# Sixteen half heads through two fixed slots, with wo in the third

## The chip, the core and the metric

The kernel runs on one core of a Trainium2 chip. The core has five engines with a queue each: TensorE (PE, with its weight loads shown as PEld), VectorE (DVE), ScalarE (ACT), GpSimd (POOL) and SyncE (SP), and sixteen transfer engines that move data between the main memory and the core. All arithmetic here is in 32-bit floats. The metric is the device time of one execution in microseconds, as the median of several.

## The reference

One decode step for 8 sequences. `x` is normalised; one branch is attention over a cache, the other a gated MLP; the result is `x + s * silu(b)`.

```python
def _A_ref(x, k_cache, v_cache, wq, wo):
    q = (x @ wq).reshape(8, 1, 32, 128)              # 32 query heads of 128
    k = repeat(k_cache, 4); v = repeat(v_cache, 4)   # 8 cached heads, 4096 positions
    p = softmax(einsum("bhqd,bhkd->bhqk", q, k) * 128 ** -0.5)
    return einsum("bhqk,bhkd->bhqd", p, v).reshape(8, 1, 4096) @ wo

def _B_ref(x, w_in, w_sp, b_sp, w_out):
    z = gelu(x @ w_in)                               # 512 -> 1792
    g = w_sp * layernorm(z[..., 896:]) + b_sp
    return (z[..., :896] * g) @ w_out

xn = layernorm(x)
return x + _A_ref(xn, ...) * silu(_B_ref(xn, ...))
```

(The transposes of the axes are left out.) The two caches have 8 x 8 x 4096 x 128 numbers each, 134 MB; `wq` and `wo` have 8.4 MB each.

## The kernel before

**Tiles and slots.** The cache of one head, of either kind, is cut into two halves of four sequences. A half is one tile of 128 partitions x 16384 numbers, 8.39 MB. There are three places for such tiles, slots a, b and c. `wq` begins in slot b and the MLP's weights in slot c; `wo` ends in slot a.

**Prologue** (L91 to L223). It loads `wq`, `x`, the MLP's weights and the first half of K (slot a), all on SP's queue; computes the queries and, once `wq` is used, loads the second half of K into slot b (L160); then it computes the MLP's gate. The head loop begins when the prologue has ended on all engines.

**The head loop.** TensorE runs `head_products` eight times in a hardware loop (L452). The other engines have their whole order written out: `head_sides` (DVE and ACT) and `loads` (SP) emit the instructions of every head one after the other. All waits are on semaphores: `pe` counts TensorE's steps (8 a head, `STEPS`), `dve` DVE's, `token` tells TensorE that DVE has got to a point (`tell`, `take`), and `landed_*` count transfers.

A head runs like this. Scores (L353): the two K tiles, from slots a and b, are multiplied with the queries; each product has a weight of 32 columns in one of four column strips of the array and 512 moving columns, and its records come in pairs, so 64 records for one tile. The queries of all heads lie in `qs`; `place_q` copies those of one head into `q`, a buffer of zeros with one window per sequence, so that the products of different sequences add up in disjoint rows of `sc`. Softmax: DVE takes the negated row maximum (`nm`), ACT exponentiates with the row sum (`l`), and since four strips of a row hold different stretches of positions, TensorE and DVE bring their maxima and sums together through a transpose (L357), a second transpose (L359) and a product with `same_all` (L361); DVE scales `p` and transposes it in blocks into `pT`. Values (L372): the V tile in slot c with the first four sequences, then the V tile in slot b with the others, into two banks `o_ps`. After each half DVE picks the diagonal blocks (`o_all`, `o_sb`) and TensorE folds them (L382) into `po`; two dummy products (L379), whose result nobody reads, stand ahead of the second fold. DVE copies `po` to `oT`, for the last head to `oT_last`.

**SP's order** in `loads`: V first half into slot c, V second half into slot b once the scores are done, the next head's first K half into slot a, and the next head's second K half into slot b once the second V half is used. Behind the last head it loads `wo` in six pieces (`WO_PIECES`, in units of 256 columns) into slot a and the rows of `x` for the output.

**The end** (`last_products`, `last_sides`). `wo` is 32 rows (head and repetition) of 512 columns. The first 28 (`FOLDED`) are multiplied in two halves of 256 columns, four rows side by side in the four strips (L408), and DVE and ACT copy one half each from PSUM into `part_sb` (L258 and L330). The products with `pick` (L430) add the four strips up into `acc`; the last four rows go to `acc` directly (L417), two of them ahead of the copies and two behind. DVE multiplies by the gate, adds `x`, and ACT stores. L258 is the line of the helper `v`, through which all of DVE's work in the loop goes; rows are told apart by their tiles.

Of the kernel before, what the change touches and what calls it, by code (L numbers as in the profile page):

```python
# [8 lines left out]
AX = mybir.AxisListType  # L9

# [4 lines left out]
G = 4  # L15
# [13 lines left out]
FOLDED = HKV * REP - REP  # L29
AHEAD = FOLDED + 2  # L30
# [3 lines left out]
STEPS = 8  # L34
WARM = 384


class Chip:


    def __init__(self, nc):
# [22 lines left out]
        self.q = sb("q", P, B * (R + REP))  # L64
# [6 lines left out]
        self.o_sb = [sb(f"o_sb{i}", P, DH) for i in range(2)]  # L71
        self.part_sb = [sb(f"part_sb{i}", P, D // 2) for i in range(2)]
# [9 lines left out]
        self.o_ps = [ps(f"o_ps{i}", P, G, DH) for i in range(2)]  # L82
        self.po_bank = ps("po", P, 512)
        self.po = self.po_bank[:, :B * REP]
# [6 lines left out]
def prologue(tc, t, x, w_mlp, wq, k0, k1, landed_a, landed_b):  # L91
# [31 lines left out]
    for z in [t.acc, *t.o_ps]:  # L123
        nc.vector.memset(z, 0.0)
# [35 lines left out]
    second = nc.sync.dma_start(slot_b, k1).then_inc(landed_b, 16)  # L160
# [65 lines left out]
def place_q(nc, t, h):  # L226
    return nc.vector.tensor_copy(t.q.rearrange("p (b s) -> p b s", b=B)[:, :, :REP], t.qs[:, h])


class Heads:  # L230
# [5 lines left out]
    def __init__(self, nc, t, landed_a, landed_b, stored):  # L236
# [3 lines left out]
        self.landed_a, self.landed_b, self.landed_c = landed_a, landed_b, nc.alloc_semaphore("landed_c")  # L240
# [4 lines left out]
        self.end = HKV * STEPS  # L245
        half_d = D // 2
        self.part = [t.sc[:, 0, :half_d], t.o_ps[0].rearrange("p g d -> p (g d)")[:, :half_d]]
# [16 lines left out]
    def loads(self, kT, v, wo, x_rows):  # L264
        sync, (a, b, c) = self.nc.sync, self.t.slots
        for h in range(HKV):
            at = h * STEPS
            if h:
                sync.wait_ge(self.pe, at - 8 + 7)
                sync.dma_start(b, kT[h, 1]).then_inc(self.landed_b, 16)  # L270
                sync.wait_ge(self.pe, at - 8 + 6)
            sync.dma_start(c, v[h, 0]).then_inc(self.landed_c, 16)
            sync.wait_ge(self.pe, at + 2)
            sync.dma_start(b, v[h, 1]).then_inc(self.landed_b, 16)
            sync.wait_ge(self.pe, at + 1)
            if h < HKV - 1:
                sync.dma_start(a, kT[h + 1, 0]).then_inc(self.landed_a, 16)
        for (lo, hi), landed in zip(WO_PIECES, self.landed_wo):
            sync.dma_start(a[:, lo * HD:hi * HD], wo[:, lo * HD:hi * HD]).then_inc(landed, 16)
        sync.dma_start(self.t.x_out, x_rows).then_inc(self.landed_x, 16)  # L280

    def head_sides(self, h):

        nc, t, at, v, vec = self.nc, self.t, h * STEPS, self.v, self.nc.vector
        p = t.p
        v(vec.tensor_reduce, t.nm, t.sc, op=ALU.max, axis=AX.XY, negate=True, pe=at + 2)
# [5 lines left out]
          op=ALU.min, axis=AX.X, pe=at + 3)  # L292
        v(vec.tensor_copy, t.full, t.nmin[:, None, :].to_broadcast([1, G, R]), own=True)
        self.tell()
        v(vec.tensor_sub, t.w, t.scr[1][:, :1], t.nm, pe=at + 4)
# [5 lines left out]
        v(vec.reciprocal, t.wl, t.scr[1][:, 1:2], pe=at + 5)  # L301
# [4 lines left out]
        if h < HKV - 1:  # L306
            vec.wait_ge(self.dve, self.nv)
            place_q(nc, t, h + 1).then_inc(self.dve, 1)
            self.nv += 1
        self.tell()  # L310
        for half in range(2):
            v(vec.tensor_mul, t.o_all, t.o_ps[half], t.diag[:, :, None].to_broadcast([P, G, DH]),
              pe=at + 6 + half)
            v(vec.tensor_reduce, t.o_sb[half], t.o_all.rearrange("p g d -> p d g"), op=ALU.add, axis=AX.X,
              own=True)
            self.tell()
        po_t = t.po.rearrange("p (b r) -> p r b", r=REP)
        if h < HKV - 1:
            v(vec.tensor_copy, t.oT[:, h], po_t, pe=at + 8)
        else:  # L320
            for a in range(2):
                v(vec.tensor_copy, t.oT_last[:, :, a, a * B:(a + 1) * B], po_t, pe=at + 8)
            self.tell()

    def last_sides(self, out):
        nc, t, vec = self.nc, self.t, self.nc.vector
        self.v(vec.tensor_copy, t.part_sb[0], self.part[0], pe=self.end + 1)
        self.tell()
        nc.scalar.wait_ge(self.pe, self.end + 2)
        nc.scalar.copy(t.part_sb[1], self.part[1]).then_inc(self.part1, 1)  # L330
        vec.wait_ge(self.act, self.na).then_inc(self.act, -self.na)
        self.v(vec.tensor_mul, t.gate, t.acc, t.gate, pe=self.end + 3)
# [5 lines left out]
        vec.wait_ge(self.pe, self.end + 3).then_inc(self.pe, -(self.end + 3))  # L338

    def take(self, sem, n):  # L340
        self.nc.tensor.wait_ge(sem, n).then_inc(sem, -n)  # L341

    def head_products(self):
        nc, t, step = self.nc, self.t, lambda mm: mm.then_inc(self.pe, 1)
        slot_a, slot_b, slot_c = t.slots
        for half, (slot, landed) in enumerate(((slot_a, self.landed_a), (slot_b, self.landed_b))):
            self.take(landed, 16)
            k_sb = slot.rearrange("p (i c g s) -> p i c g s", i=HALF, c=2, g=G)
            for i in range(HALF):
                b = half * HALF + i  # L350
                for c in range(2):
                    for g in range(G):
                        mm = nc.tensor.matmul(t.sc[R * g:R * (g + 1), c, :], t.q[:, b * R:(b + 1) * R],  # L353
                                              k_sb[:, i, c, g, :], start=(b == 0), stop=(b == B - 1))
# [139 lines left out]
```

## Time and profile before

| | |
|---|---|
| median of 3 runs | 678.85 us (678.63 to 678.86) |
| profiled execution | 679.39 us, of which its span is 678.1 us |
| moved by the transfer engines | 290.9 MB, 429 GB/s over the span |
| first scores on TensorE | from 61.5 us |
| last product on values, end | 665.2 us |
| store issued | 676.6 us |
| mean granted TensorE clock | 0.75 of full |

The page gives each engine's busy time and share, then the span in 40 slices: a digit is the busy share of an engine in tenths, PEclk the clock that TensorE was granted, GB/s what the transfers moved. A timeline row has the start, the duration, the engine, the line and the operation with its tiles, a count where several are merged, and in brackets the idle time ahead of it with what ended it. A group row has busy time and mean ns of one, then the idle time ahead. A row of a stretch has its bounds and length, busy time and count of PE, PEld, DVE, ACT and POOL, then granted clock, DMA share and GB/s. A transfer row has size and the median time from issue to landing. "issue" and "PEq" name an engine's own sequencer: where TensorE waits for a semaphore in its queue, for a landing above all, the idle time is written down to it.

### The profile page before, as it was taken

Reading aid. Unit: us, or ns where it says so; the run is one execution under the profiler, and the core shown is the slowest. Engines: PE = TensorE matmul, PEld = TensorE weight load, DVE = VectorE, ACT = ScalarE, POOL = GpSimd, SP = SyncE. Lnnn points to the kernel's source line nnn. Section 1 sums busy time; section 2 is a strip of 40 time slices with the busy share of each in tenths; the row PEclk is TensorE's granted clock in tenths of the full one; section 3 lists DMA queues with packets and bytes.
Section 4 is the critical chain, followed back from the end, with each engine's and each line's share of the span. In section 5 each row is a group of like instructions: output and inputs, shape, how many; then the busy total and the mean of one; then the engine's idle time right before and its main releaser. Section 6 shows DMA issues by size and latency. Waiting matters only on the chain. (4 is left out here: it accounts for less than half of the span.)

```text
span 678.1 us, 5431 instructions
## 1 busy us (share of the span) xinstructions
PE 351.0 (52%) x2480; PEld 102.7 (15%) x2480; DVE 80.7 (12%) x156; ACT 13.8 (2%) x28; POOL 2.8 (0%) x15
## 2 busy tenths in 40 slices
PE   0446743545565444456555444655645454655548
PEld 0112210111121111111111110111111111211104
DVE  0142021102110021101100021101101021100111
ACT  0010000000000000000000000000000000000000
POOL 1000000000000000000000000000000000000000
PEclk9986766778767677877766677887666678877659
DMA  9999999999999999999999999999999999999996
GB/s 383 439 433 434 434 433 433 434 433 433 433 433 433 433 433 433 437 437 437 445 437 433 437 437 433 441 437 433 433 433 433 433 433 433 433 433 433 433 414 287
DMA packets 6070, 290.90 MB, mean 429 GB/s; under 512 B 936, under 2 KB 1064, under 8 KB 1456
## 3 DMA queue, kind: packets, MB, share of 16 engines
q1 hardware_dynamic: 5920, 290.79, 99.1%
q8 instruction: 4, 0.07, 0.0%
q10 hardware_dynamic: 144, 0.03, 0.0%
q14 instruction: 2, 0.02, 0.0%
HBM read 290.78 MB, written 0.03 MB: 429 GB/s over the span
## 5 line engine op out<-in xcount | busy, mean ns | idle before, releaser
L372 PE MATMUL o_ps<-slot_b,pT 128*16 128x512 f32 x512 | 74.9, 751 | 81.0 <-PEq L341 81.0
L353 PE MATMUL sc<-slot_b,q 128*32 128x512 f32 x512 | 74.4, 746 | 73.5 <-PEq L341 73.5
L353 PE MATMUL sc<-slot_a,q 128*32 128x512 f32 x512 | 75.5, 756 | 56.2 <-PEq L341 56.2
L372 PE MATMUL o_ps<-slot_c,pT 128*16 128x512 f32 x512 | 73.9, 742 | 47.9 <-PEq L341 47.9
L258 DVE TENSOR_REDUCE nm<-sc 128x1 f32<-128x1024 f32 x8 | 9.8, 1225 | 277.0 <-PE sc L353 277.0
L258 DVE TENSOR_TENSOR o_all<-o_ps,diag 128x512 f32<-128x512 f32 x16 | 11.1, 692 | 243.4 <-PE o_ps L372 243.4
L353 PEld LDWEIGHTS sc<-slot_b,q 128*32 128x32 f32 x512 | 20.4, 134 | 127.5 <-issue 127.5
L372 PEld LDWEIGHTS o_ps<-slot_b,pT 128*16 128x16 f32 x512 | 17.6, 114 | 138.4 <-issue 138.4
L353 PEld LDWEIGHTS sc<-slot_a,q 128*32 128x32 f32 x512 | 20.7, 135 | 104.7 <-issue 104.7
L372 PEld LDWEIGHTS o_ps<-slot_c,pT 128*16 128x16 f32 x512 | 17.4, 114 | 97.7 <-issue 97.7
L289 ACT ACTIVATE p<-sc,nm 128x1024 f32<-128x1024 f32 x8 | 8.9, 1114 | 554.4 <-DVE nm L258 554.4
L258 DVE TENSOR_REDUCE o_sb<-o_all 128x128 f32<-128x512 f32 x16 | 16.4, 1025 | 0.5
L142 PE MATMUL scr<-ident,slot_c 8*128 8x8 f32 x4 | 0.6, 255 | 25.2 <-DVE slot_c L139 25.2
L379 PE MATMUL scr<-pT,ident 128*128 128x384 f32 x32 | 12.3, 507 | 0.0
L258 DVE STREAM_TRANSPOSE pT<-p 128x1024 f32<-128x1024 f32 x8 | 10.0, 1245 | 0.3
L150 PE MATMUL scr<-slot_b,xnT 128*32 128x512 f32 x64 | 9.0, 717 | 0.3 <-DVE xnT L143 0.3
L357 PE MATMUL scr<-ident,nm 128*1 128x128 f32 x8 | 2.2, 269 | 11.9 <-PEq L341 11.9
L382 PE MATMUL po<-fold,o_sb 128*128 128x16 f32 x32 | 6.1, 266 | 2.5 <-PEq L341 2.5
L361 PE MATMUL scr<-wl,same 128*128 128x1 f32 x16 | 3.6, 297 | 6.6 <-PEq L341 6.6
L382 PEld LDWEIGHTS po<-fold,o_sb 128*128 128x128 f32 x32 | 4.8, 188 | 14.0 <-issue 14.0
L258 DVE TENSOR_SCALAR p<-p,w,wl 128x1024 f32<-128x1024 f32 x8 | 6.5, 813 | 0.3
L379 PEld LDWEIGHTS scr<-pT,ident 128*128 128x128 f32 x32 | 5.5, 191 | 2.1
(92 smaller groups left out, 77.9 us busy)
## 6 DMA issues: line engine op xcount, KB each, us to landing
slot_c<-in_w_mlp SPq DMA_DIRECT2D x1, 5392.0 KB, 33.8
slot_a<-in_wo SPq DMA_DIRECT2D x1, 4608.0 KB, 40.1
slot_a<-in_wo SPq DMA_DIRECT2D x1, 2048.0 KB, 44.5
slot_a<-in_wo SPq DMA_DIRECT2D x2, 512.0 KB, 45.7
slot_a<-in_wo SPq DMA_DIRECT2D x1, 384.0 KB, 46.7
slot_a<-in_kT SPq DMA_DIRECT2D x8, 48.1
slot_b<-in_kT SPq DMA_DIRECT2D x8, 29.2
slot_c<-in_v SPq DMA_DIRECT2D x8, 48.1
```

The source lines that it names most:

```text
L142: nc.tensor.transpose(pt[:, k * B:(k + 1) * B], xn[:, k * P:(k + 1) * P], t.ident[:B, :B])
L150: nc.tensor.matmul(pq[R * g:R * (g + 1), :], t.xnT[:, k, :], wq_sb[:, k, lo:lo + REP * DH], start=(k == 0), stop=(k == NK - 1))
L258: make(*args, **kw).then_inc(self.dve, 1)
L289: nc.scalar.activation(p, t.sc.rearrange("p c s -> p (c s)"), AF.Exp, bias=t.nm, accum_out=t.l).then_inc(self.act, 1)
L353: mm = nc.tensor.matmul(t.sc[R * g:R * (g + 1), c, :], t.q[:, b * R:(b + 1) * R], k_sb[:, i, c, g, :], start=(b == 0), stop=(b == B - 1))
L357: step(nc.tensor.transpose(t.scr[0][:1, :P], t.nm, t.ident))
L361: step(nc.tensor.matmul(t.scr[1][:, 1:2], t.same_all, t.wl, start=True, stop=True))
L372: mm = nc.tensor.matmul(of[R * i:R * i + G * REP, :], pT[:, j, half * HALF + i], v_sb[:, i, j], start=(j == 0), stop=(j == J - 1))
L379: nc.tensor.matmul(t.scr[1][:, :WARM], t.ident, pT.rearrange("p j b x -> p (j b x)")[:, :WARM], start=True, stop=True)
L382: mm = nc.tensor.matmul(t.po[:, half * n:(half + 1) * n], t.o_sb[half], t.fold.rearrange("p i r -> p (i r)"), start=True, stop=True)
```

## The change

The loop goes over sixteen units, each a head's half: one K tile and one V tile, with a softmax of its own over the four sequences in it. K always goes to slot a and V to slot b; the prologue's second cache tile is now V0. Slot c holds the MLP's weights and then only `wo`. The query windows have 16 columns instead of 32, so half of the rows of `sc` are zeros that the prologue sets. Dummy products, now 512 columns wide, stand after the scores, after the second transpose, in a loop of five before the values, and two before the fold. `wo` is folded 512 wide for 30 rows instead of 256 wide for 28; DVE and ACT copy 64 partitions each of the sum, and only then come `pick` and the last two rows.

```diff
-FOLDED = HKV * REP - REP
-AHEAD = FOLDED + 2
+FOLDED = HKV * REP - 2
-STEPS = 8
-WARM = 384
+UNITS = HKV * 2
+STEPS = 6
+Q = HALF * REP
...
-        self.q = sb("q", P, B * (R + REP))
+        self.q = sb("q", P, HALF * (Q + REP))
...
-    for z in [t.acc, *t.o_ps]:
+    for z in [t.sc, t.acc, t.o_ps, t.part]:
         nc.vector.memset(z, 0.0)
...
-    second = nc.sync.dma_start(slot_b, k1).then_inc(landed_b, 16)
+    second = nc.sync.dma_start(slot_b, v0).then_inc(landed_b, 16)
...
     def loads(self, kT, v, wo, x_rows):
         sync, (a, b, c) = self.nc.sync, self.t.slots
-        for h in range(HKV):
-            at = h * STEPS
-            if h:
-                sync.wait_ge(self.pe, at - 8 + 7)
-                sync.dma_start(b, kT[h, 1]).then_inc(self.landed_b, 16)
-                sync.wait_ge(self.pe, at - 8 + 6)
-            sync.dma_start(c, v[h, 0]).then_inc(self.landed_c, 16)
-            sync.wait_ge(self.pe, at + 2)
-            sync.dma_start(b, v[h, 1]).then_inc(self.landed_b, 16)
-            sync.wait_ge(self.pe, at + 1)
-            if h < HKV - 1:
-                sync.dma_start(a, kT[h + 1, 0]).then_inc(self.landed_a, 16)
+        for u in range(1, UNITS):
+            at = (u - 1) * STEPS
+            sync.wait_ge(self.pe, at + 1)
+            sync.dma_start(a, kT[u // 2, u % 2]).then_inc(self.landed_a, 16)
+            sync.wait_ge(self.pe, at + 5)
+            sync.dma_start(b, v[u // 2, u % 2]).then_inc(self.landed_b, 16)
         for (lo, hi), landed in zip(WO_PIECES, self.landed_wo):
-            sync.dma_start(a[:, lo * HD:hi * HD], wo[:, lo * HD:hi * HD]).then_inc(landed, 16)
+            sync.dma_start(c[:, lo * HD:hi * HD], wo[:, lo * HD:hi * HD]).then_inc(landed, 16)
...
     def last_sides(self, out):
-        self.v(vec.tensor_copy, t.part_sb[0], self.part[0], pe=self.end + 1)
+        self.tell()
+        self.v(vec.tensor_copy, t.part_sb[:P // 2], t.part[:P // 2], pe=self.end + 1)
         self.tell()
-        nc.scalar.wait_ge(self.pe, self.end + 2)
-        nc.scalar.copy(t.part_sb[1], self.part[1]).then_inc(self.part1, 1)
+        nc.scalar.wait_ge(self.pe, self.end + 1)
+        nc.scalar.copy(t.part_sb[P // 2:], t.part[P // 2:]).then_inc(self.part1, 1)
...
+    def warm(self):
+        t = self.t
+        self.nc.tensor.matmul(t.scr[1], t.ident, t.ident[:, None, :].to_broadcast([P, D // P, P]),
+                              start=True, stop=True)
+
+    def unit_products(self):
+        nc, t, step = self.nc, self.t, self.step
+        slot_a, slot_b, _ = t.slots
+        self.take(self.landed_a, 16)
+        k_sb = slot_a.rearrange("p (i c g s) -> p i c g s", i=HALF, c=2, g=G)
+        for i in range(HALF):
+            for c in range(2):
+                for g in range(G):
+                    mm = nc.tensor.matmul(t.sc[R * g:R * g + Q, c, :], t.q[:, i * Q:(i + 1) * Q],
+                                          k_sb[:, i, c, g, :], start=(i == 0), stop=(i == HALF - 1))
+        step(mm)
+        self.warm()
+        self.take(self.token)
+        step(nc.tensor.transpose(t.scr[0][:1, :P], t.nm, t.ident))
+        self.take(self.token)
+        step(nc.tensor.transpose(t.scr[0][:, P:P + 1], t.full.rearrange("b g r -> b (g r)"), t.ident[:1, :1]))
+        self.warm()
+        self.take(self.token)
+        step(nc.tensor.matmul(t.scr[0][:, P + 1:P + 2], t.same_all, t.wl, start=True, stop=True))
+        with nc.tensor.Fori(0, 5):
+            self.warm()
+        self.take(self.token)
+        self.take(self.landed_b, 16)
+        pT = t.pT.rearrange("p j b g r -> p j b (g r)")
+        v_sb = slot_b.rearrange("p (i j e) -> p i j e", i=HALF, j=J)
+        of = t.o_ps.rearrange("p g d -> p (g d)")
+        for j in range(J):
             for i in range(HALF):
...
+                mm = nc.tensor.matmul(of[R * i:R * i + Q, :], pT[:, j, i], v_sb[:, i, j],
+                                      start=(j == 0), stop=(j == J - 1))
         step(mm)
+        self.take(self.token)
+        for _ in range(2):
+            self.warm()
+        self.take(self.token)
+        step(nc.tensor.matmul(t.po, t.o_sb, t.fold.rearrange("p i r -> p (i r)"), start=True, stop=True))
...
     def last_products(self):
+        wo_sb = t.slots[2].rearrange("p (m d) -> p m d", d=D)
...
+        for m in range(FOLDED):
+            need(2 * m + 2)
+            h, r = divmod(m, REP)
+            if m == (HKV - 1) * REP:
+                self.take(self.token)
+            o = t.oT[:, h, r, :] if h < HKV - 1 else t.oT_last[:, r, 0, :B]
+            mm = nc.tensor.matmul(t.part[R * r:R * r + B, :], o, wo_sb[:, m, :],
+                                  start=(m < REP), stop=(m >= FOLDED - REP))
+        step(mm)
...
+        self.take(self.token)
+        self.take(self.part1)
         for a in range(2):
             for g in range(G):
-                c = (2 * (g % 2) + a) * W
+                c = (2 * g + a) * W
                 nc.tensor.matmul(t.acc[R * g:R * g + OUT_ROWS, :], t.pick[:, a, :OUT_ROWS],
-                                 t.part_sb[g // 2][:, c:c + W], start=False, stop=False)
-        for m in range(AHEAD, HKV * REP):
+                                 t.part_sb[:, c:c + W], start=(a == 0), stop=False)
+        for m in range(FOLDED, HKV * REP):
...
-    with nc.tensor.Fori(0, HKV):
-        heads.head_products()
-    heads.last_products()
+    with nc.tensor.Fori(0, UNITS):
+        units.unit_products()
+    units.last_products()
```

More of the change, by code (lines that the diff above doesn't have):

```diff
@@ L70, in __init__ @@
         self.oT_last = sb("oT_last", P, REP, 2, OUT_ROWS)
-        self.o_sb = [sb(f"o_sb{i}", P, DH) for i in range(2)]
-        self.part_sb = [sb(f"part_sb{i}", P, D // 2) for i in range(2)]
+        self.o_sb = sb("o_sb", P, DH)
+        self.part_sb = sb("part_sb", P, D)
         self.o_all = sb("o_all", P, G, DH)
@@ L81, in __init__ @@
         self.sc = ps("sc", P, 2, 512)
-        self.o_ps = [ps(f"o_ps{i}", P, G, DH) for i in range(2)]
+        self.o_ps = ps("o_ps", P, G, DH)
+        self.part = ps("part", P, D)
         self.po_bank = ps("po", P, 512)
-        self.po = self.po_bank[:, :B * REP]
+        self.po = self.po_bank[:, :Q]
         self.acc_bank = ps("acc", P, 512)
@@ L244, in __init__ @@
         self.nv = self.na = 0
-        self.end = HKV * STEPS
-        half_d = D // 2
-        self.part = [t.sc[:, 0, :half_d], t.o_ps[0].rearrange("p g d -> p (g d)")[:, :half_d]]
+        self.end = UNITS * STEPS
     def v(self, make, *args, own=False, pe=None, act=None, **kw):
```

138 lines of the change are left out of this document (39 added, 99 removed).

## The prediction, made before the changed kernel ran

> **What bounds the kernel now.** I read the page's slices first, to see which resource never rests.
>
> ```profile
> span 678.1 us, 5431 instructions
> PE 351.0 (52%) x2480; PEld 102.7 (15%) x2480; DVE 80.7 (12%) x156; ACT 13.8 (2%) x28; POOL 2.8 (0%) x15
> ...
> DMA  9999999999999999999999999999999999999996
> GB/s 383 439 433 434 434 433 433 434 433 433 433 433 433 433 433 433 437 437 437 445 437 433 437 437 433 441 437 433 433 433 433 433 433 433 433 433 433 433 414 287
> ```
>
> No engine is busy for more than 52% of the span, while the transfer engines are at 9 in every slice but the last and move 433 GB/s almost throughout. Then the table of stretches, the TensorE timeline and SyncE's timeline, which show how regular this is:
>
> ```profile
> 75.41 9.75 PE L353 MATMUL sc<-slot_b,q 128*32 128x512 f32 x64 [4.02 <-PEq L341]
> ...
> 86.65 0.27 PE L357 MATMUL scr<-ident,nm 128*1 128x128 f32 x1 [1.49 <-PEq L341]
> ...
> 88.75 0.56 PE L361 MATMUL scr<-wl,same 128*128 128x1 f32 x2 [0.83 <-PEq L341]
> 94.86 8.55 PE L372 MATMUL o_ps<-slot_c,pT 128*16 128x512 f32 x64 [5.55 <-PEq L341]
> 114.17 9.13 PE L372 MATMUL o_ps<-slot_b,pT 128*16 128x512 f32 x64 [10.76 <-PEq L341]
> ```
> ```profile
> 85.21 0.33 SPq L274 DMA_DIRECT2D slot_b<-in_v  x1
> 85.59 0.44 SPq L277 DMA_DIRECT2D slot_a<-in_kT  x1
> 123.36 0.33 SPq L270 DMA_DIRECT2D slot_b<-in_kT  x1
> ```
> ```profile
> 152.70:616.70 464.00, 241.79 (x1608) 67.95 (x1609) 48.42 (x84) 8.45 (x18) 0.00 (x0) 0.73 1.00 434
> ```
>
> Each 8.39 MB tile reaches TensorE 19.3 us after the one before it (75.41, 94.86, 114.17), is used up in about 9 to 10 us, and then TensorE idles. The last row covers six heads, 24 tiles: 464.0 / 24 = 19.33 us per tile, DMA share 1.00. So the time is the sum of the transfers, plus a start before TensorE matters and an end after the last transfer. An edit can matter only in two ways: it lets the transfer engines run dry, or it alters the end.
>
> **The change part by part.**
>
> *The tile order and slots.* The bytes do not change: 16 K tiles, 16 V tiles, wq, the MLP weights and wo. The order becomes K0, V0, K1, V1 and so on, with K always in slot a and V in slot b. A transfer now waits for the previous tile of its own kind. What counts is its lead: how long before the tile in flight is seen by TensorE the next transfer is issued. Take K(u) seen at 0, so V(u) is seen at 19.3 and K(u+1) at 38.6. The scores of one unit have the same 64 records as one old half, at most 9.9 us (row at 61.53 below); 16 weight columns instead of 32 change nothing, because the V products above already have 16 and run at the same pace. K(u+1) is issued at 9.9: a lead of 9.4 us before V(u). PV(u) runs from 19.3 to 29.2 at worst (the 9.91 us row in the end below): V(u+1) has again a lead of 9.4 us before K(u+1). How much is needed?
>
> ```profile
> slot_b<-in_wq SPq DMA_DIRECT2D x1, 21.9
> ```
>
> That transfer started with nothing in flight and took 21.9 us, so start-up and landing cost at most 21.9 - 19.3 = 2.6 us. And the existing kernel already lives on such leads: at 85.21, one tile was in flight, seen at 94.86 (lead 9.65), and the next was still seen 19.31 us later. Leads of 9.4 against 2.6 leave 6.8 us. Cost 0; without the cover every us of lateness costs 15 times, once for each refill of that slot.
>
> *The first unit* is tighter, since TensorE starts late:
>
> ```profile
> 61.53 9.86 PE L353 MATMUL sc<-slot_a,q 128*32 128x512 f32 x64 [2.65 <-PEq L341]
> ```
> ```profile
> 64.06 0.23 PEld L353 LDWEIGHTS sc<-slot_a,q 128*32 128x32 f32 x4 [0.63 <-issue]
> 64.92 0.23 PEld L353 LDWEIGHTS sc<-slot_a,q 128*32 128x32 f32 x4 [0.63 <-issue]
> ...
> 69.06 0.14 PEld L353 LDWEIGHTS sc<-slot_a,q 128*32 128x32 f32 x4 [0.29 <-issue]
> 69.49 0.14 PEld L353 LDWEIGHTS sc<-slot_a,q 128*32 128x32 f32 x4 [0.29 <-issue]
> ```
> ```profile
> 61.50:67.20 5.70, 5.67 (x28) 1.58 (x32) 0.00 (x0) 0.00 (x0) 0.00 (x0) 0.50 0.93 402
> 67.20:71.40 4.20, 4.19 (x40) 1.08 (x32) 0.00 (x0) 0.00 (x0) 0.00 (x0) 1.00 1.15 499
> ```
>
> V0 takes the place of the second K tile in the prologue, behind the same waits, and is seen at 75.4. Scores of unit 0 end at 61.53 + 9.86 = 71.39, K1 is issued then, and the lead is 4.0 us against 2.6: cost 0, with 1.4 us to spare. Four records take 0.86 us at a granted clock of 0.50 and 0.43 at 1.00. If all 64 ran at 0.50 they would take 13.7 us, end at 75.2, and K1 would come 2.4 us late. I take 0, because here the clock rose after 5.7 us.
>
> *Sixteen softmaxes for eight.* One softmax on TensorE goes from the end of the scores (75.41 + 9.75 = 85.16) to the L361 row (88.75): 3.6 us; then DVE scales and transposes. Eight more of these, and eight more L258 rows of each kind, lie under the wait for V(u). Without that cover they would cost 8 x 3.6 = 29 us and more.
>
> ```profile
> 89.55 0.81 DVE L258 TENSOR_SCALAR p<-p,w,wl 128x1024 f32<-128x1024 f32 x1
> 90.40 1.25 DVE L258 STREAM_TRANSPOSE pT<-p 128x1024 f32<-128x1024 f32 x1
> ```
>
> *Dummy products.* Per unit: one after the scores, one after the second transpose, five in a loop before the token for PV, two before the fold. Each is two records of 128x512 on the whole array. The trace has such products only 384 wide:
>
> ```profile
> 665.41 1.54 PE L379 MATMUL scr<-pT,ident 128*128 128x384 f32 x4
> ```
>
> 0.385 us per record, so by width 0.51, and 1.0 us per dummy product at full clock, 2.0 at half. The first hides in the 1.49 us that TensorE idles ahead of L357, the second exceeds the 0.83 us ahead of L361 by 0.2. With L361 itself (0.56) and the loop (5 x 1.02), PV is then ready at 9.9 + 3.6 + 0.2 + 0.6 + 5.1 = 19.4 us, just when V(u) arrives. At half clock throughout the first two show 0.5 and 1.2 and the loop takes 10.2: 9.9 + 3.6 + 0.5 + 1.2 + 0.6 + 10.2 = 26.0, PV would end at 35.9, and V(u+1) would have a lead of 2.7 us, still the 2.6 needed. The loop's own branches have no row; from 0 to 1 us per pass, by the 0.83 us that TensorE takes from token to product at L361. I take 0, because the outer loop's wait on data has always covered its branch.
>
> *wo in slot c.* Its pieces are still issued behind the last V tile, which is issued when PV(14) ends. V14 arrives when the last second K tile arrived before, so this is near the old 625.5: no move.
>
> *The end* is where the sum is not 0.
>
> ```profile
> 636.02 9.32 PE L372 MATMUL o_ps<-slot_c,pT 128*16 128x512 f32 x64 [6.64 <-PEq L341]
> ...
> 655.32 9.91 PE L372 MATMUL o_ps<-slot_b,pT 128*16 128x512 f32 x64 [9.98 <-PEq L341]
> ...
> 667.64 0.62 PE L408 MATMUL sc<-slot_a,oT 128*8 128x256 f32 x8
> ...
> 673.91 0.38 PE L408 MATMUL o_ps<-slot_a,oT 128*8 128x256 f32 x1
> ...
> 674.33 0.42 DVE L258 COPY part_sb<-sc 128x256 f32<-128x256 f32 x1 [6.38 <-PE o_ps L408]
> 674.39 0.37 ACT L330 COPY part_sb<-o_ps 128x256 f32<-128x256 f32 x1 [45.76 <-PE o_ps L408]
> 675.08 0.27 PEld L430 LDWEIGHTS acc<-part_sb,pick 128*16 128x16 f32 x16 [0.52 <-issue]
> ...
> 676.04 0.23 DVE L258 TENSOR_TENSOR gate<-acc,gate 128x64 f32<-128x64 f32 x1 [1.28 <-PE acc L417]
> ```
> ```profile
> 625.90 2.80 SPq L279 DMA_DIRECT2D slot_a<-in_wo  x6
> ```
> ```profile
> slot_a<-in_wo SPq DMA_DIRECT2D x2, 512.0 KB, 45.7
> slot_a<-in_wo SPq DMA_DIRECT2D x1, 384.0 KB, 46.7
> ...
> slot_a<-in_wo SPq DMA_DIRECT2D x1, 128.0 KB, 46.4
> ```
> ```profile
> L178 DVE COPY p<-scr 128x512 f32<-128x512 f32 x1 | 0.7, 693 | 3.4 <-PE scr L175 3.4
> ...
> L182 ACT ACTIVATE p<-p 128x512 f32<-128x512 f32 x1 | 0.6, 630 | 0.0
> ```
>
> Today 28 of 32 rows of wo are folded, the fold ends at 674.29, two copies of 256 columns end at 674.76, and L430 starts at 675.08. Now 30 are folded, so the fold needs the fourth piece. The six issues are 0.47 us apart; the fourth leaves at 627.3 and lands after 45.7 to 46.7 us, at about 673.4. Products start 0.1 later, at 673.5. Rows 28 and 29 go side by side, two records one behind the other: 0.43 + 0.6 = 1.0 us, so the fold ends at 674.5. By work it isn't later: 28 rows are 56 records of 512 columns, 14 x 0.43 = 6.0 us, and from 667.64 that is 673.6. The copies are 512 columns wide on half the partitions: DVE 0.69 (row L178), ACT 0.63 (L182), so they end at 674.5 + 0.10 + 0.65 = 675.3 rather than 674.76. What follows, 16 records of L430 and 32 of L417, is unchanged. The end moves by 675.3 - 674.76, **0.5 us**. The lower bound is the last piece: sixth issue 628.25 + 46.4 = 674.65, plus 0.2 and eight records (0.2), so the gate could start at 675.1 and not 676.04, **0.9 us** less. The upper bound is the half-clock case above: PV of the last unit would start 26.0 us after K15 is seen (where the third tile of the last head is seen today, 636.0), at 662.0 rather than 655.3; after 10 us of loop at most 6.9 us for it, 2.5 to the fold (665.2 to 667.64 today), 6.0 and 1.0 for the fold: 678.4, **3.9 us** over 674.5. I take +0.5, which goes by measured landings.
>
> **Sum.** 0 + 0 + 0 + 0.5 on a span of 678.1 gives 678.6. The profiled execution took 679.39 us; the median of the runs is 678.85, 0.54 lower; from the median: 679.4.
>
> **The rivals.**
> *A, loop too long (slower).* The five dummy products run at half clock, or their loop branches are slow, so the last PV starts after V15 is there. It decides from 19.3 us after K15 is seen; each us costs one us at the end, up to 683. Past 26 us V refills come late too, 15 us for each us. For it: DVE has pT ready at 91.65, 2.3 us after L361, so the loop's 5.1 us end last. Against: TensorE has just run scores for 9.9 us and reached 1.00.
> *B, first refill late (slower).* Unit 0 stays at half clock: 2.4 us, 681.2. For it: only 1.4 us to spare. Against: the 0.50 and 1.00 rows. [...]
> *C, a shallow queue pays every start-up (slower).* With one transfer queued, 30 refills x 2.6 = 78 us, 757. Against: the seamless refill issued at 85.21. [...]
> *D, a shorter end.* The last V product meets a warmer TensorE and the copies hide: 678.0, still within no change.
>
> **How the numbers follow.** Forecast 0.80 (own range 678.6 to 680.1), A 0.08, B 0.04, C 0.02, D 0.06. The range goes from D's 678.0 to 681.2, which takes in B and the low end of A and leaves out some 0.08. A measurement of this kernel tells about 0.2%, 1.4 us, from no change. Faster by that would need more than D's bound: 0.02. Slower: most of A, B's upper half and C, with a little for a late fold: 0.12. Within: 0.86.
>
> **What would show it.** Right: a rhythm of 19.3 us from K to V to K, GB/s at 433 in every slice, K and V issues some 9 us ahead, K1 issued near 71.4, part copies of 0.6 to 0.7 us that end near 675.3. A: a PV whose wait ends in TensorE's own queue and not with a landing. B: a dip of DMA share near 73 to 77. C: dips at every tile. Wrong altogether: a rhythm over 19.4 us, or an end that moves by over 1.4 us.

## The result, and the profile after

| | before | after |
|---|---|---|
| median of 6 runs | 678.78 us (678.63 to 679.1) | 681.68 us (681.18 to 685.07) |
| ratio, 95% interval | | 1.005 (1.0031 to 1.007) |
| profiled execution, its span | 679.39, 678.1 us | 685.07, 682.8 us |

The changed kernel is 2.9 us slower, above the top of the forecast range. The execution that was profiled is the slowest of its six, so everything below is compared with further executions too. The profile page of the changed kernel begins so:

```profile
span 682.8 us, 6217 instructions
PE 449.7 (66%) x2684; PEld 138.8 (20%) x2684; DVE 118.7 (17%) x238; ACT 25.3 (4%) x52; POOL 2.6 (0%) x15
...
GB/s 392 424 431 430 428 442 445 445 434 430 434 430 430 434 430 434 426 434 430 434 427 434 430 430 453 449 434 434 430 430 430 430 434 430 434 434 430 427 429 197
```

SyncE's timeline of the first unit, with the issues of K1 and V1:

```profile
71.74 0.33 SPq L273 DMA_DIRECT2D slot_a<-in_kT  x1
87.03 0.33 SPq L275 DMA_DIRECT2D slot_b<-in_v  x1
```

TensorE's timeline, at the first unit, at two places further on and at the last unit:

```profile
63.13 8.55 PE L356 MATMUL sc<-slot_a,q 128*16 128x512 f32 x64 [2.66 <-PEq L338]
...
75.44 4.54 PE L345 MATMUL scr<-ident 128*128 128x512 f32 x10
79.91 7.06 PE L376 MATMUL o_ps<-slot_b,pT 128*16 128x512 f32 x64
96.97 8.69 PE L356 MATMUL sc<-slot_a,q 128*16 128x512 f32 x64 [7.61 <-PEq L338]
...
329.18 8.64 PE L356 MATMUL sc<-slot_a,q 128*16 128x512 f32 x64 [9.87 <-PEq L338]
349.53 8.71 PE L376 MATMUL o_ps<-slot_b,pT 128*16 128x512 f32 x64 [3.41 <-PEq L338]
...
619.79 7.06 PE L376 MATMUL o_ps<-slot_b,pT 128*16 128x512 f32 x64 [1.49 <-PEq L338]
640.10 8.49 PE L356 MATMUL sc<-slot_a,q 128*16 128x512 f32 x64 [10.86 <-PEq L338]
659.39 8.76 PE L376 MATMUL o_ps<-slot_b,pT 128*16 128x512 f32 x64 [2.50 <-PEq L338]
```

The third tile of the loop (K1 now, the first V tile before) is seen at 96.97, not at 94.86: 2.1 us are lost in the first unit. From there to the last tile lie 29 tiles: 659.39 - 96.97 = 562.42 us, where before it was 655.32 - 94.86 = 560.46. These 2.0 us are mostly in two places: nearly every step is 19.3 us, a few up to 19.5, but 329.18 to 349.53 is 20.35 and 619.79 to 640.10 is 20.31. The kernel before has one longer step too, of 19.74:

```profile
558.38 8.89 PE L372 MATMUL o_ps<-slot_c,pT 128*16 128x512 f32 x64 [5.17 <-PEq L341]
578.12 9.26 PE L372 MATMUL o_ps<-slot_b,pT 128*16 128x512 f32 x64 [10.85 <-PEq L341]
```

Every one of these tiles is waited for; TensorE is never what is late. Last, the end:

```profile
670.55 4.46 PE L401 MATMUL part<-slot_c,oT 128*8 128x512 f32 x36
...
675.17 2.75 PE L401 MATMUL part<-slot_c,oT 128*8 128x512 f32 x20 [0.16 <-PEq L338]
...
677.74 1.03 PE L401 MATMUL part<-slot_c,oT_last 128*8 128x512 f32 x4
678.81 0.58 ACT L327 COPY part_sb<-part 64x512 f32<-64x512 f32 x1 [27.07 <-PE part L401]
678.81 0.68 DVE L262 COPY part_sb<-part 64x512 f32<-64x512 f32 x1 [7.99 <-PE part L401]
...
679.85 0.42 PE L417 MATMUL acc<-part_sb,pick 128*16 128x64 f32 x16 [1.08 <-PEq L338]
...
680.77 0.23 DVE L262 TENSOR_TENSOR gate<-acc,gate 128x64 f32<-128x64 f32 x1 [1.27 <-PE acc L408]
```

From the end of the last data packet of `wo` (678.35 after, 674.35 before) to the end of the span it takes 4.45 us; before it was 3.75. So this execution lost 2.1 + 2.0 + 0.7 = 4.8 us in its span (682.8 - 678.1 = 4.7), in three places.

The view of the transfers, cut to the loop (62 to 655 us), shows what else changed. The row with q14, of the kind `instruction`, counts blocks of 8 KB (8192 bytes each in the packet record). That they are program, the view says by this name alone; the experiments below try it. First the kernel before (count, MB, share of sixteen engines):

```profile
q8 instruction: 2, 0.03, 0.0%
q14 instruction: 2, 0.02, 0.0%
```

And in the changed kernel:

```profile
q8 instruction: 1, 0.02, 0.0%
q14 instruction: 3, 0.02, 0.0%
```

The row with q8 counts blocks of 16 KB; one of them, with the row behind it, takes its engine back by some 1.4 us (at 80.81 in the kernel before: 0.95 for the block and 2.90 instead of 2.42 for the row). The kernel before has one more of these, so the bytes of this kind that arrive in the loop are not more now (40 KB against 48); what matters is which transfer engine a block falls on.

By the packet record the blocks of 8 KB arrive at 83.5, 348.0 and 633.8 us in the changed kernel, and the two long steps are those in which the second and the third fall. In the kernel before they arrive at 97.7 and 559.8 us, and the second falls in the step of 19.74. They come over the same sixteen transfer engines as the tiles. The record does not name the engines, but each packet begins where the one ahead of it on its engine ends, to within 0.01 us, so they can be followed: all three blocks of the changed kernel fall on one engine, both of the kernel before on one, and the blocks of 16 KB on others. The same view, cut to 633.7 to 634.3 us, has the third block alone:

```profile
q1 hardware_dynamic: 3, 0.13, 56.0%
q14 instruction: 1, 0.01, 3.2%
```

Its share is 3.2% of 16 x 0.6 us, 0.31 us on one engine, and in the packet record that engine's next 64 KB row takes some 2.95 us instead of 2.42: together 0.85 us late. TensorE begins a tile when the slowest of sixteen is done with it (the engines end V15 at 653.61 to 658.82 us, and its products begin at 659.39; in the kernel before the last V tile ends at 652.80 to 654.81, and they begin at 655.32), and by the same record each engine carries eight rows of 64 KB of every tile, so such a delay isn't made up if it falls on the engine that is already last. In the changed kernel the engine that takes the three blocks is the last one from K1 on: it carries K1 when the first block comes, so 0.85 of the 2.1 us lost there are that block's. In the kernel before, the engine that takes the first block is ahead of the last by more than 0.85 us, the tiles show nothing, and only the second block makes it the last.

### The profile page after: what moved, and what is told of

The parts are those of the page before. It is cut to its first block, busy times and chain, and to the rows that moved or that the text cites. A ratio compares the mean times of both kernels' runs of the same rounds, so it can differ in the third digit from the quotient of the medians.

```text
span 682.8 us, 6217 instructions
## 1 busy us (share of the span) xinstructions
PE 449.7 (66%) x2684; PEld 138.8 (20%) x2684; DVE 118.7 (17%) x238; ACT 25.3 (4%) x52; POOL 2.6 (0%) x15
## 5 line engine op out<-in xcount | busy, mean ns | idle before, releaser
L356 PE MATMUL sc<-slot_a,q 128*16 128x512 f32 x1024 | 145.9, 734 | 141.1 <-PEq L338 141.1
L376 PE MATMUL o_ps<-slot_b,pT 128*16 128x512 f32 x1024 | 123.1, 636 | 29.0 <-PEq L338 29.0
L345 PE MATMUL scr<-ident 128*128 128x512 f32 x288 | 140.2, 614 | 0.0
L356 PEld LDWEIGHTS sc<-slot_a,q 128*16 128x16 f32 x1024 | 34.4, 112 | 239.4 <-issue 239.4
L262 DVE TENSOR_REDUCE nm<-sc 128x1 f32<-128x1024 f32 x16 | 19.6, 1225 | 283.1 <-PE sc L356 283.1
L345 PEld LDWEIGHTS scr<-ident 128*128 128x128 f32 x288 | 49.5, 189 | 65.7 <-issue 65.5
L376 PEld LDWEIGHTS o_ps<-slot_b,pT 128*16 128x16 f32 x1024 | 33.3, 101 | 117.3 <-issue 117.3
L287 ACT ACTIVATE p<-sc,nm 128x1024 f32<-128x1024 f32 x16 | 17.8, 1113 | 561.4 <-DVE nm L262 561.4
L262 DVE STREAM_TRANSPOSE pT<-p 128x1024 f32<-128x1024 f32 x16 | 19.9, 1245 | 0.6
L401 PE MATMUL part<-slot_c,oT 128*8 128x512 f32 x56 | 7.2, 593 | 0.2 <-PEq L338 0.2
```

Source lines behind the costliest of these rows:

```text
L262: make(*args, **kw).then_inc(self.dve, 1)
L287: nc.scalar.activation(p, t.sc.rearrange("p c s -> p (c s)"), AF.Exp, bias=t.nm, accum_out=t.l).then_inc(self.act, 1)
L345: self.nc.tensor.matmul(t.scr[1], t.ident, t.ident[:, None, :].to_broadcast([P, D // P, P]), start=True, stop=True)
L356: mm = nc.tensor.matmul(t.sc[R * g:R * g + Q, c, :], t.q[:, i * Q:(i + 1) * Q], k_sb[:, i, c, g, :], start=(i == 0), stop=(i == HALF - 1))
L376: mm = nc.tensor.matmul(of[R * i:R * i + Q, :], pT[:, j, i], v_sb[:, i, j], start=(j == 0), stop=(j == J - 1))
L401: mm = nc.tensor.matmul(t.part[R * r:R * r + B, :], o, wo_sb[:, m, :], start=(m < REP), stop=(m >= FOLDED - REP))
```

## The experiments

The theories at the start. **First refill**: K1's issue at 71.74 is too late for the transfer engines to go on without a gap (rival B's place). **Program**: DVE's written-out program is longer, needs a third block, and the slowest transfer engine pays for it. **End**: the new end costs more than the 0.5 us of the sum. Rival to all three: the profiled execution is merely an unlucky one. Each median below stands beside that of the kernel before in runs on the same chip.

**The changed kernel again**, unaltered.

> The changed kernel itself, a second profile beside its repeats, since its first profiled execution (685.07 us) is 3.4 us above the median of its runs (681.68). All theories: a median of 681.2 to 682.2. Theory F (the first refill comes late): the second K tile is seen by TensorE at 95.5 to 97.5 us and not at 94.9 as the third tile before. Theory N (the end alone): the rhythm is unbroken from V0 on, K1 is seen at 94.9, and the whole loss lies behind the last landing.

Median 681.6 (681.2 to 683.42, 5 runs) against 678.81: ratio 1.0039 (1.0026 to 1.0052). The loss is no accident. In this execution K1 is seen at 95.71 and V15 at 657.55, 561.84 us apart, and the span ends 4.4 us after the last packet of `wo`. The last two losses repeat at 1.4 and 0.7, the first varies.

**The old end.** 28 rows folded, two rows ahead of the copies; the fold and the copies stay 512 wide.

```diff
-FOLDED = HKV * REP - 2
+FOLDED = HKV * REP - REP
+AHEAD = FOLDED + 2
...
+        for m in range(FOLDED, AHEAD):
+            for a in range(2):
+                direct(m, a, lambda g: (2 * g + a) * W, start=(m == FOLDED and a == 0))
+        self.take(self.token)
```

> The changed kernel with 28 rows of wo folded and two rows taken directly ahead of the copies, as before the change; the copies stay 512 wide. Theory N (the end): the copies no longer wait for the fourth piece, so from the last landing to the end it takes 3.7 us again and not 4.5: 0.7 us off, a median near 681.0; if the end were the whole loss, 678.8. Theory F alone: unchanged, 681.7.

Median 680.72 (680.26 to 682.33, 5 runs), ratio 1.0033 (1.0021 to 1.0046): 0.9 us of the 2.8 come back by the medians, and the end takes 3.6 us after the last packet of `wo`. The intervals overlap, but four of the five executions lie below all eleven of the changed kernel.

**Refilling K in halves**, so that K1's first half is issued when half of the scores are done: TensorE counts that in a new semaphore `mid`, which SyncE takes back at the very end. K0 is loaded in halves too.

```diff
+            sync.wait_ge(self.mid, u)
+            sync.dma_start(a[:, :SLOT // 2], k[:, :SLOT // 2]).then_inc(self.landed_a, 16)
             sync.wait_ge(self.pe, at + 1)
-            sync.dma_start(a, kT[u // 2, u % 2]).then_inc(self.landed_a, 16)
+            sync.dma_start(a[:, SLOT // 2:], k[:, SLOT // 2:]).then_inc(self.landed_a, 16)
```

> The changed kernel with each K tile refilled in two transfers of half a tile, the first as soon as TensorE is half through the scores; nothing else. K1's first half is then issued near 67.5 us, 8 us ahead of V0's arrival and not 3.9. Theory F: no transfer engine runs dry at V0 to K1, K1 is seen at 94.9 to 95.2, and the time falls by 1 to 2 us, to 679.7 to 680.7. Theory N: unchanged, 681.7.

Median 682.29 (681.9 to 682.7, 5 runs), ratio 1.0053 (1.004 to 1.0066): slower, though K1 (first issue at 68.39) is seen at 94.88. What a lead can mend, it mends; but the rest of the loop takes 561.74 us and the end is the long one. So the first refill can't be the whole loss.

**The kernel before with a late first refill**: its first V tile is issued when the scores of K0 are done.

```diff
                 sync.wait_ge(self.pe, at - 8 + 6)
+            else:
+                sync.wait_ge(self.pe, 1)
             sync.dma_start(c, v[h, 0]).then_inc(self.landed_c, 16)
```

> The kernel before the change with one wait more: the first V tile is issued only when the first half of the first scores is done, near 71.4 us and not at 61.25, so that its lead over the tile in flight is 4 us, as K1's is in the changed kernel. Theory F: the third cache tile is seen 0.5 to 2.2 us later than 94.9 and the time rises to 679.5 to 681.0. Theory N: no change, 678.8.

Issued at 71.20 instead of 61.25. Median 679.42, but spread from 678.61 to 681.36 in 12 runs, where the kernel before, in 17 runs, stays within 678.46 and 679.58; ratio 1.0014 (1.0004 to 1.0023). Four runs lie at 678.6 to 678.8, four at 679.2 to 679.8, four at 680.7 to 681.4. The same issue time thus costs nothing in one execution and 2.5 us in another. In the profiled one the tile was seen at 94.83, in time.

**K1 later still** in the changed kernel: it waits for the next step, some 1.3 us on.

```diff
-            sync.wait_ge(self.pe, at + 1)
+            sync.wait_ge(self.pe, at + (2 if u == 1 else 1))
```

> The changed kernel with the issue of K1 alone put off by one step of TensorE, from the end of unit 0's scores to the transpose behind them: 1.5 to 1.8 us later, near 73.2. Theory F (the lead of the first refill has run out): K1 is seen 1 to 2 us later than 94.9 in every execution and the median rises from 681.6 to 682.5 to 683.5. If the lead in the changed kernel were as ample as the prediction had it (4.0 against 2.6), only 0.2 to 0.4 us would be lost: 681.8.

Issued at 73.04; median 682.68 (682.1 to 683.94, 5 runs) against 678.89, ratio 1.0058 (1.0044 to 1.0071): 1.0 us over the changed kernel by the medians for 1.3 us of delay. All five executions lie above eight of the changed kernel's eleven, and K1 is seen at 96.34. There is hardly any spare time at this place.

**Fewer DVE instructions** in the changed kernel: where DVE tells TensorE something, the instruction that produces it raises the token, instead of an empty signal behind it. That takes 4 empty instructions out of every unit, 64 in all, and moves no work; TensorE waits for one signal less.

```diff
-        v(vec.tensor_copy, t.full, t.nmin[:, None, :].to_broadcast([1, G, R]), own=True)
-        self.tell()
+        v(vec.tensor_copy, t.full, t.nmin[:, None, :].to_broadcast([1, G, R]), own=True, to_pe=True)
```

> The changed kernel with four of DVE's six pure signal instructions per unit left out: the instruction ahead of each signals TensorE itself, or a later signal covers it; same arithmetic, 64 instructions fewer on DVE. Theory R (the doubled, written-out softmax makes DVE's program longer, each 8 KB refill of it delays the transfer engine that carries it by 0.85 us, and the delays of one engine add up to the end): two refills of 8 KB between 60 and 655 us and not three, the last V tile seen 0.8 to 1.0 us earlier against K1, the median down by 0.9 to 680.7. Without R: 681.6.

Median 680.88 (680.72 to 682.66, 7 runs), ratio 1.0029 (1.0018 to 1.004), against 1.0039 and 1.005 for the changed kernel: 0.7 to 0.8 us by the medians. The intervals overlap, but six of the seven executions lie below all eleven of the changed kernel. The span gained more than the time: its median is 678.7 us, against 680.3 in the second set of the changed kernel, while each of the seven executions takes 2.0 to 2.6 us beyond its span (see Open). Its transfers in the loop:

```profile
q14 instruction: 2, 0.02, 0.0%
```

And its TensorE timeline:

```profile
95.99 9.95 PE L355 MATMUL sc<-slot_a,q 128*16 128x512 f32 x64 [6.60 <-PEq L337]
...
618.07 7.06 PE L375 MATMUL o_ps<-slot_b,pT 128*16 128x512 f32 x64 [1.64 <-PEq L337]
637.37 8.92 PE L355 MATMUL sc<-slot_a,q 128*16 128x512 f32 x64 [9.91 <-PEq L337]
```

The third block is gone, and so is the step of 20.3 us at the end of the loop (618.07 to 637.37 is 19.30); the 29 tiles take 560.69 us.

**The kernel before with more DVE instructions**: 16 empty signals after every head's transpose, 128 in all, at a place where DVE waits anyway (13.38 us in the kernel before, ahead of its row at 181.32).

```diff
+        for _ in range(16):
+            vec.wait_ge(self.dve, self.nv).then_inc(self.pad, 1)
```

> The kernel before the change with 128 empty signal instructions more on DVE, 16 for each head, at a place where DVE idles for some 10 us; nothing else. Theory R: three refills of 8 KB in place of two before 655 us, the last V tile seen 0.85 us later, the median up from 678.8 to 679.6. Without R: 678.8.

Median 679.82 (679.29 to 680.68, 11 runs) against 678.89: ratio 1.0013 (1.0004 to 1.0022), 0.93 us. Its transfers in the loop:

```profile
q14 instruction: 3, 0.02, 0.0%
```

And its TensorE timeline:

```profile
326.68 9.45 PE L376 MATMUL o_ps<-slot_c,pT 128*16 128x512 f32 x64 [6.51 <-PEq L345]
346.43 9.82 PE L376 MATMUL o_ps<-slot_b,pT 128*16 128x512 f32 x64 [10.29 <-PEq L345]
...
616.76 9.49 PE L357 MATMUL sc<-slot_b,q 128*32 128x512 f32 x64 [10.40 <-PEq L345]
637.11 9.54 PE L376 MATMUL o_ps<-slot_c,pT 128*16 128x512 f32 x64 [6.71 <-PEq L345]
```

One block more, and steps of 19.75 and 20.35 us appear where the kernel before has 19.3; the second and the third block arrive at 330.5 and 635.6, in these same steps. Instructions that do nothing, put where DVE waits, lengthen the run by 0.93 us, where the theory had 0.85 for one block.

**Old end and fewer instructions together.**

> The changed kernel with both edits: the fold of 28 rows with two direct rows ahead of the copies, and 64 signal instructions fewer on DVE. The first alone brought 681.6 to 680.7. Theories N and R together: 679.8, and what stays over 678.8 is the first refill and the wider copies. If the two gains are the same one (the end hidden by the late engine): 680.7.

Median 679.37 (678.98 to 682.33, 11 runs), ratio 1.0014 (1.0005 to 1.0023). Beside the old end alone that is 1.35 us for the instructions, beside the fewer instructions alone 1.5 us for the end. What is left is 0.5 us and a spread: 5 of 11 runs lie over 680, and in the profiled one, at 682.33, K1 is seen at 97.14.

**The same with K in halves**, and with the `mid` semaphore taken back as it goes.

> The changed kernel with three edits: 28 rows folded, 64 signal instructions fewer on DVE, and K refilled in halves with SyncE taking the new count back as it goes and not at the end. The first two alone gave 679.4, with single executions between 679.0 and 682.3. Theory F (the first refill is late in some executions and not in others): K1 seen near 94.9 and the spread gone, 678.9 to 679.4 with no execution over 680. If the spread has another cause: 679.4 with the same spread.

Median 680.05, but all 11 runs within 679.9 to 680.26; ratio 1.0017 (1.0008 to 1.0026). K1's first half is issued at 67.63, 4.1 us earlier than the whole in the changed kernel, and the spread is gone. The median is higher by 0.7. SyncE's own program has grown, and a third block is back at 630.9 us; that the block is SyncE's is likely, as the next run has one more there too, but the trace doesn't name its owner. Nor do the 29 tiles show the 0.7 (561.05 against 560.96), so its cause stays open.

**K in halves, taken back as it goes**, with nothing else.

> The changed kernel with K refilled in halves, as in the earlier run that came out at 682.3, but with the new count taken back by SyncE as it goes and no wait at the very end. If that run lost by the wait at the end what the early refill gained: 680.9 to 681.4, below the changed kernel's 681.6. If the halves themselves cost (more packets, more issues): 682.3 again.

Median 682.0 (681.74 to 682.2, 5 runs), ratio 1.0046 (1.0032 to 1.0059): like the first form in halves, with four blocks in the loop. The halves give back what they gain.

**Fewer DVE instructions in the kernel before**, 5 a head. ACT's exponential then waits for the transpose behind the maximum and not for the maximum.

> The kernel before the change with five of DVE's seven pure signal instructions per head left out, 40 in all; same arithmetic. Theory R: the second of its two 8 KB refills no longer falls before 655 us, the last V tile is seen 0.7 to 0.9 us earlier, and the time falls from 678.85 to 678.0 to 678.2, below both kernels. Without R: 678.85.

Median 678.81 (678.37 to 679.23, 11 runs) against 678.96: ratio 0.9996 (0.9987 to 1.0005). The view of transfers shows one block instead of two, yet there is hardly a gain, so the expectation of a whole block's price failed.

```profile
q14 instruction: 1, 0.01, 0.0%
```

The packet record says why that can be: at the end of the kernel before, its slowest transfer engine is 2.01 us behind the fastest, and others are as much as 1.74 behind. Taking a block from the slowest only makes the next one the last, 0.27 us earlier. The trace of this run agrees: at the last V tile the engine that took the block is not among the last three, and two of those had taken a block of 16 KB.

**Warming TensorE for the first scores**: old end, fewer instructions, and four dummy products at the end of the prologue.

```diff
+    for _ in range(4):
+        nc.tensor.matmul(t.scr[turn[0] ^ 1], t.ident, t.ident[:, None, :].to_broadcast([P, D // P, P]),
+                         start=True, stop=True)
```

> The changed kernel with the 28-row fold and 64 signals fewer on DVE (679.4, single executions from 679.0 to 682.3), and four dummy products more behind the prologue's last product, while TensorE waits for the end of the prologue: the first scores then run at full clock, 7 us and not 8.5 to 10, and K1 is issued 1.5 to 3 us earlier, near 69, with not one instruction more on SyncE or DVE. Theory F: K1 seen near 94.9 in the profiled execution and no execution over 680, median 679.0 to 679.2. If the spread isn't F: 679.4 with executions up to 682.

The first scores take 7.06 us instead of 9.92, and K1 is issued at 70.09 instead of 71.77. Median 679.45 (679.2 to 681.01, 11 runs), ratio 1.0013 (1.0004 to 1.0022): the median did not fall, but the spread went from 3.35 to 1.8 us. A lead longer by 1.7 us takes out the worst executions only.

**The new end alone, in the kernel before**: 512 wide, 30 rows.

```diff
+        for m in range(FOLDED):
+            need(2 * m + 2)
+            ...
+            mm = nc.tensor.matmul(self.part[R * r:R * r + B, :], o, wo_sb[:, m, :],
+                                  start=(m < REP), stop=(m >= FOLDED - REP))
```

> The kernel before the change with the changed kernel's end alone: wo folded 512 wide for 30 rows, copies of 64 partitions x 512, then the last two rows. Theory N: from the landing of the last piece to the end of the span 4.4 us and not 3.7, 0.5 (as the prediction had it) to 0.9 us slower: 679.3 to 679.7. If the price of that end in the changed kernel came from its late transfers alone: 678.85.

Median 680.24 (680.07 to 680.98, 11 runs) against 678.85: ratio 1.002 (1.0011 to 1.0029), 1.4 us. Its end in the timeline:

```profile
667.37 6.56 PE L400 MATMUL sc<-slot_a,oT 128*8 128x512 f32 x56
...
673.82 1.03 PE L400 MATMUL sc<-slot_a,oT_last 128*8 128x512 f32 x4
674.89 0.58 ACT L328 COPY part_sb<-sc 64x512 f32<-64x512 f32 x1 [44.84 <-PE sc L400]
674.89 0.68 DVE L256 COPY part_sb<-sc 64x512 f32<-64x512 f32 x1 [7.21 <-PE sc L400]
...
676.85 0.23 DVE L256 TENSOR_TENSOR gate<-acc,gate 128x64 f32<-128x64 f32 x1 [1.28 <-PE acc L407]
```

The 28 rows take 6.56 us without a wait, so this fold is bound by TensorE. The gate starts at 676.85 instead of 676.04.

All profiled executions side by side: the blocks that arrive in the loop, and the time of the 29 tiles, from the third tile of the loop as TensorE sees it to the last.

| blocks of 8 KB | kernels | 29 tiles, us |
|---|---|---|
| 1 | before, fewer instructions | 560.52 |
| 2 | before; before, late refill; before, new end | 560.46; 560.38; 560.74 |
| 2 | after, fewer instructions; with old end; with warm start | 560.69; 560.96; 560.32 |
| 3 | before, more instructions | 561.39 |
| 3 | after; again; old end; late K1; halves | 562.42; 561.84; 561.39; 561.74; 561.74 |
| 3 | all changes with halves | 561.05 |
| 4 | after, halves taken back | 561.95 |

The two groups don't overlap: up to two blocks, 560.58 on the mean of seven; three or four, 561.69 on the mean of eight; but the nearest two are 0.09 us apart. The count stands for the delays of one engine and is not the whole cause: in the versions of the changed kernel the first block (80.6 to 84.1 us) falls ahead of the 29 tiles, so the unaltered one has two inside them, as many as the kernel before. Whether these show depends on how far the engine that takes them was behind the others by then.

No version beats both kernels: the nearest, the kernel before with fewer instructions, can't be told from it.

## Why the prediction was wrong, step by step

**Right: the rhythm.** Two fixed slots with one transfer ahead keep the engines busy: 19.3 us per tile except for the steps above, and rival C, a start-up paid at every tile, is refuted. Rival A is too: PV of unit 0 (its product with V) starts 16.8 us after its scores (63.13 to 79.91), before the tile is due 19.3 after the last one, and PV of unit 15 ends its idle time of 2.50 us with a landing. Ten dummy records take 4.54 us where the sum had 5.1. D, a shorter end, is refuted by the last experiment: the end is longer.

**Wrong: "sixteen softmaxes for eight ... lie under the wait".** Their run time does. The step priced instructions by duration and left out that each is also some 64 bytes (an estimate, from the spacing below) of a program that is written out for every unit and fetched during the run, through the engines that bound the kernel. Removing 64 of them without moving work gave 0.7 to 1.35 us, adding 128 to the kernel before cost 0.93. By the traces DVE has 21 instructions a head before and 37 with the empty ones, 18 a unit after and 14 with fewer, at 77.3 us a head and 38.66 a unit (four and two tiles of 19.33). The blocks are 462, 235 and 305, 265 and 286, and 344 us apart, which is 126, 112 and 146, 123 and 133, and 125 instructions: 128 on the mean of the six, and 8 KB over 128 is 64 bytes. The page of before already had the row with two blocks in its queues; nothing of it was in the sum.

**Wrong in part: "the first unit ... cost 0, with 1.4 us to spare".** The place was rival B's, its reason wasn't. TensorE did not stay at half clock through the first scores: they took 8.55 us, less than the 9.86 before, at a granted clock of 0.64 up to 67.40 and 1.00 from there. But they began 1.6 us later (63.13), so K1 was issued at 71.74 rather than 71.39, and above all the need was not 2.6 us. That bound came from a transfer that started with nothing in flight. Under load, in the profiled execution, fourteen engines began K1 at 73.2 to 73.7 by the packet record, as they were done with V0, and one at 75.10, when it was; the last, done with V0 at 73.49, began only at 75.97, 4.2 us after the issue. So the last engine, free 1.75 us after the issue, stood idle for another 2.5. In the profiled executions of after and its variants K1 is 0 to 2.3 us late. The kernel before with such a lead spreads over 2.75 us, and in three versions of the changed kernel the spread shrinks with the lead: 3.35 us at an issue at 71.8, 1.8 at 70.1, 0.36 with a first half at 67.6. Why one engine starts late in some executions stays open.

**Too small: the end, "+0.5".** The direction was right. Two parts can be seen in the last experiment: the copies take 0.68 against 0.42, as the sum had it, but the fold ends at 674.85 (673.82 + 1.03), not 674.5, since 56 records take 6.56 us where the sum had 14 x 0.43 = 6.0. So the fold is not set by the fourth landing, and the profile shows 0.8 us (676.85 - 676.04). The medians show 1.4 when it is put in, 0.9 and 1.5 when it is taken out. Of the 0.6 us between, 0.5 is that the profiled execution of before lies that much over its median.

**The sum as it should have been**: by what each cost in the kernel before, 0.9 (a block) + 1.4 (the end) leaves 0.6 of the measured 2.9 for the first refill, a remainder that no run measured alone. How the loss is split is not firm. By median spans, taking the instructions out of the changed kernel gains 1.6 us (680.3 to 678.7), or 1.4 beside the old end (679.4 to 678.0); taking the new end out gains 0.9 (680.3 to 679.4) or 0.7 (678.7 to 678.0). What is left of the span is 0.5 over the kernel before (677.5), and that holds the wider copies too.

**Open.** Part of the loss lies outside the span. The time is 1.3 to 1.6 us over the span in every execution of the kernel before for which both were taken, and 1.3 to 1.4 us in six of the changed kernel's eleven, but 1.9 to 2.5 in the other five and 2.0 to 2.6 in all seven with fewer instructions. In three of the profiled executions (the two of the unaltered changed kernel and the one with fewer instructions) a refill of 16 KB stands behind the end of the span, at 684.1, 682.3 and 681.4 us, and there the difference is 2.3 to 2.5; in the twelve others that block lies within the span, and it is 1.3 to 1.6. So part of what the old end gained beside fewer instructions, 1.5 us of time for 0.7 of span, may be this block; no run tried it alone. Why taking out 64 instructions gains more span than the 0.85 us of one block is open too.

## What to carry to other kernels

Where transfers set the time, count instructions as bytes too: here the orders that are written out came with blocks of 8 KB during the run, over the same transfer engines, and a block that fell on the engine that was already last cost its whole 0.85 us. Bound a lead by how late the slowest transfer engine has started under load (here 4.2 us after the issue), and take a spread of executions as a sign that it may be short (3.35 us here, 0.36 with an issue 4.1 us earlier). Bound the end of a kernel by the work of its engine (here 6.56 us for 56 records) as well as by the landing that it waits for.

## What was not expected of the hardware

A refill of 8 KB costs its transfer engine 0.85 us, nearly three times its own 0.31, and the delay of the slowest engine stayed to the end of the kernel: in the profiled execution of the changed kernel one engine, which began K1 2.5 us after it was free, was hit by all three blocks and was 5.2 us behind the fastest at V15, while from K1 to V15 (97 to 655 us) the mean was 433 GB/s and the DMA share 1.00. So a share of 1.00 does not show that tiles come at their fastest: the mean over sixteen engines hides the one that everything waits for.
